# Second stages issued two slots later, and six more tiles by seven products, in a spectral-mixing and squared-ReLU kernel

## The chip, the cores and the metric

One Trainium2 chip; the kernel runs on one of its cores. The metric is the device time of one execution in microseconds (us), the median of several. Names of engines in the profile: PE is TensorE's matmul and PEld its weight load, DVE is VectorE, ACT is ScalarE, POOL is GpSimd, SP is the engine whose queue issues most transfers.

## The reference

```python
batch, seq, dim = (8, 3008, 256); d_ff = 2048
X = np.fft.rfft(x, axis=1);  Xr, Xi = X.real, X.imag
Yr = Xr @ w_r - Xi @ w_i + b_r
Yi = Xr @ w_i + Xi @ w_r + b_i
Yr = sign(Yr) * maximum(abs(Yr) - 0.01, 0);  Yi likewise
y = np.fft.irfft(Yr + 1j * Yi, n=3008, axis=1)
h = y.reshape(24064, 256) @ moe_w_in          # 256 -> 2048
r = maximum(h, 0)
out = (moe_s * (r * r) + moe_b) @ moe_w_out   # 2048 -> 256
```

## The kernel before

The first half (the transform along the sequence, the mixing, the shrinking and the transform back) is done by matmuls with constant tables, batch by batch, in units: s1 (first transform step, exits `u`), s23 (second step, mixing, shrink, first step back, exits `xf`, `ring`, `v`) and s4 (last step, exits `yt`). Between the steps data goes through HBM: `ud`, `us`, `vd`, `vs`, and the `ring` is filled by small transfers. The exits from PSUM are copies (L187 on ScalarE, L189 on VectorE).

The second half works on 48 tiles of up to 512 rows of `y` (`_tile_order`): six "wide" ones for each of batches 0 and 1, then five "main" ones per later batch, with "tail" tiles of a pair of batches between them. `mark[b] // MC` is the number of batch b's first tile, called m below: 12, 17, 23, 29, 35 and 41 for batches 2 to 7.

A tile has 16 slots (`MC`), one for each 128 of the 2048 columns. `first_mm` issues in each slot the two matmuls of `y @ w_in`, 512 columns each, into a bank of `psh`. After every second slot ScalarE takes two banks by ReLU into `rt` (L871), and `rt * rt` goes as fp16 into `gt`, on VectorE (L884) or ScalarE (L881). A planner decides which: `act_first` (L180) compares the work that it has booked on both, and it places most exit copies in the same way. `gt` has four buffers, two to a tile: `q=0` holds the squares of slots 0 to 7, `q=1` those of slots 8 to 15.

The second stage of a tile, `r * r @ w_out`, is issued beside the first stage of the next tile, slot by slot. There are two forms:

- `second_mms`: four row blocks of 128 by 16 steps, 64 matmuls of 256 columns, four to a slot; one exit for two blocks (L945).
- `seven_mms`: the rows of the tile, the columns of `w_out` and the 2048 are each halved, and the 2 x 2 block product is made from seven block products in place of eight (order index 0 to 6), 112 matmuls of 128 columns, seven to a slot. The tables `T_s` hold sums of the blocks of `w_out`. The sums of blocks of `gt` are made for each half q by `s_op`, in place: n=1 adds a21 and a22 into `s1`, n=3 puts a11 - a21 over a21, n=2 takes `s1` from a11, n=4 adds a11 to a12 with an accumulating DMA from POOL's queue (L973). The first three are on VectorE (L980). Product 3 reads `s1`, 4 the new a11, 5 the new a21, 6 the new a12. The products share PSUM banks in pairs; a tile uses four banks one after the other, and `psa` has two (in the last batch `psa` and `psf` in turn). `leave(group)` empties them on VectorE (L1012, and L1030 for one sum): group 0 after products 0 and 1, group 1 after 2, group 2 after 3 and 4, group 3 after 5 and 6. Each is one to three additions scaled by `s_bc`.

`seven(ti)` says which tiles take the second form: 17 of the 48, the two ahead of each m, three of batch 0 and 1, and the last batch's but for the tiles that are too narrow or last.

The final loop is the order of issue: in each slot the units that `plan` holds for it (s1, s23, s4 units and loads), then `first_mm`, then the second-stage matmuls of the tile before. A scheduler then moves instructions by a few places on each engine. Every engine works through its own list in order. POOL's list holds the loads of `x`, the accumulating DMAs and a copy of tails (L805).

Of the kernel before, what the change touches and what calls it, by code (L numbers as in the profile page):

```python
# [11 lines left out]
ALU = mybir.AluOpType  # L12
# [84 lines left out]
def kernel(  # L97
# [14 lines left out]
    B, S, D = x.shape  # L112
# [4 lines left out]
    MC = DFF // P  # L117
# [54 lines left out]
    def matmul(out, lhs, rhs, **how):  # L172
        if pe["on"]:
            pe["now"] += 0.0025 + int(np.prod(rhs.shape[1:])) / 2400.0
        return nc.tensor.matmul(out, lhs, rhs, **how)  # L175
# [35 lines left out]
    def sum_bank(ti):  # L211
        return any_bank() if ti >= mark[B - 1] // MC else other_bank()
# [602 lines left out]
    def sub_size(tl):  # L815
        return 4 * tl[3] if tl[0] == "wide" else P
# [105 lines left out]
    def second_mms(ti):  # L922

        tl = tiles[ti]
        size = sub_size(tl)
        nsub = -(-tl[3] * (16 if tl[0] == "wide" else 1) // size)
        hold = {}

        def mm(sub, mc):

            alone = ti == len(tiles) - 1 and sub >= 2
            h = 0 if alone else sub % 2
            if h == 0 and mc == 0:
                hold["ps"] = sum_bank(ti).rearrange("p (h e) -> p h e", h=2)
            ps = hold["ps"]
            matmul(
                ps[0:size, h, :],
                lhs_of(ti, mc, sub),
                w_out_t[:, mc, :],
                start=(mc == 0), stop=(mc == MC - 1),  # L940
            )
            if mc == MC - 1 and (alone or h == 1 or sub == nsub - 1):
                k = h + 1
                ost = opool.tile([P, 2, D], F32, name="ost", tag="ost")
                nc.vector.scalar_tensor_tensor(  # L945
                    out=ost[0:size, 0:k], in0=ps[0:size, 0:k], scalar=s_bc[0:size],
                    in1=bias_bc[0:size].unsqueeze(1).to_broadcast([size, k, D]), op0=ALU.mult, op1=ALU.add,
                )
# [12 lines left out]
    def part(ti, q, i, k):  # L961
        size = 2 * sub_size(tiles[ti])
        return gts[(ti, q)][:, i, k, :, 0:size]

    def s_op(ti, n, q):

        size = 2 * sub_size(tiles[ti])
        if n == 1:
            sums[(ti, q)] = spool.tile([P, 4, 2 * P], F16, name="s1", tag="s1")
        s1 = sums[(ti, q)][:, :, 0:size]  # L970
        a11, a12, a21, a22 = (part(ti, q, i, k) for i in range(2) for k in range(2))
        if n == 4:
            nc.gpsimd.dma_start(out=a12, in_=a11, accum_op=ALU.add)  # L973
            return
        out, a, b, op = {
            1: (s1, a21, a22, ALU.add),
            3: (a21, a11, a21, ALU.subtract),
            2: (a11, a11, s1, ALU.subtract),
        }[n]
        nc.vector.tensor_tensor(out=out, in0=a, in1=b, op=op)  # L980
        work("dve", 0.07 + size / 480.0)

    def seven_mms(ti):

        tl = tiles[ti]
        size = sub_size(tl)
        hold = {}
        left = [(0, 0), (0, 1), (1, 1), None, (0, 0), (1, 0), (0, 1)]
        firsts = (0, 2, 3, 5)
        T = T_s[0]  # L990
        right = [w_block(0, 0), w_block(1, 0), T[:, 3], T[:, 0], T[:, 1], T[:, 2], w_block(1, 1)]

        def mm(n, j, c):

            if n in firsts and j == 0 and c == 0:
                hold["ps"] = sum_bank(ti).rearrange("p (n j e) -> p n j e", n=2, j=2)
            if j == 0 and c == 0:
                hold[n] = hold["ps"][0:size, 0 if n in firsts else 1]
            q, g = divmod(c, 4)
            at = slice(j * size, (j + 1) * size)  # L1000
            if left[n] is None:
                lhs = sums[(ti, q)][:, g, at]
            else:
                lhs = gts[(ti, q)][:, left[n][0], left[n][1], g, at]
            matmul(
                hold[n][:, j], lhs, right[n][:, c],
                start=(n in firsts and j == 0 and c == 0), stop=(c == MC // 2 - 1),
                skip_group_check=True,
            )

        def add(out, of, other):
            nc.vector.scalar_tensor_tensor(  # L1012
                out=out, in0=of, scalar=s_bc[0:size], in1=other, op0=ALU.mult, op1=ALU.add
            )
            work("dve", 0.4)

        def wide(t):
            return t[0:size, 0:P].unsqueeze(1).to_broadcast([size, 2, P])

        def leave(group):  # L1020
            if group == 0:
                hold["z"] = zpool.tile([P, 2, 2, P], F32, name="zz", tag="zz")
            if group in (0, 3):
                hold["o", group] = opool.tile([P, 2, D], F32, name="ost", tag="ost")
            z = hold["z"][0:size]
            top = hold["o", 0][0:size]
            if group == 0:
                add(z[:, 0], hold[0], wide(bias_bc))
                add(top[:, :, 0:P], hold[1], z[:, 0])
                nc.vector.tensor_tensor(out=z[:, 1], in0=z[:, 0], in1=wide(b_21), op=ALU.add)  # L1030
                work("dve", 0.34)
            elif group == 1:
                add(z[:, 0], hold[2], z[:, 0])
            elif group == 2:
                add(z[:, 1], hold[3], z[:, 1])
                two = hold[4].rearrange("p j e -> p (j e)").unsqueeze(1).to_broadcast([size, 2, D])
                zs = z.rearrange("p h j e -> p h (j e)")
                add(zs, two, zs)
# [12 lines left out]
        order = [  # L1051
            (n, j, c) for h in range(2) for n in range(early) for j in range(2)
            for c in range(4 * h, 4 * h + 4)
        ]
        order += [(n, j, c) for n in range(early, 6) for j in range(2) for c in range(C)]
        order += [(6, j, c) for h in range(2) for j in range(2) for c in range(4 * h, 4 * h + 4)]
        slots = [[] for _ in range(MC)]
        for at, what in enumerate(order):
            slots[at // 7].append(lambda w=what: mm(*w))
        for at, n, q in ((2, 2, 0), (2, 1, 1), (2, 4, 0), (3, 3, 1), (4, 2, 1), (5, 4, 1)):  # L1060
            at += alone and at > 3
            slots[at].append(lambda n=n, q=q: s_op(ti, n, q))
        for at, group in ((4 + alone, 0), (6, 1), (11, 2), (15, 3)):
            slots[at].append(lambda group=group: leave(group))
        return slots

    def seven(ti):
        if ti >= len(tiles) - 2 or not halves(ti):
            return False
        firsts = [mark[b] // MC for b in range(2, B)]  # L1070
        return (
            ti >= firsts[-1] or 4 <= ti < 7 or any(m - 2 <= ti < m for m in firsts)
        )

    plan = {}
# [18 lines left out]
    mark = {}  # L1094
# [13 lines left out]
    for b in range(2, B):  # L1108
        s0, s1, s2 = mark[b - 2], mark[b - 1], mark[b]
        p = s1 - s0  # L1110
        units, take_rows = s1_units(b)
# [4 lines left out]
        units, take_half = s23_units(b)  # L1116
# [7 lines left out]
                )  # L1124

    ti_n = len(tiles)
    for ti in range(ti_n + 1):
        nxt = [[]] * MC
        if ti:
            nxt = seven_mms(ti - 1) if seven(ti - 1) else second_mms(ti - 1)  # L1130
        for mc in range(MC):
            if ti < ti_n:
                for u in plan.pop(ti * MC + mc, []):
                    u()
                first_mm(ti, mc)
                if mc in (10, 11) and seven(ti):
                    s_op(ti, 1 if mc == 10 else 3, 0)
            for u in nxt[mc]:
                u()
    assert not plan  # L1140


# [28 lines left out]
```

## Time and profile before

| what | value |
|---|---|
| median of 3 runs (lowest to highest) | 838.71 us (838.18 to 838.87) |
| the profiled execution | 838.19 us |
| its span, first to last instruction | 836.4 us |
| granted TensorE clock | 1.000 |
| chain that ended last: PE, DVE, ACT, DMA | 81%, 8%, 5%, 3% |
| `rt` by ReLU on ScalarE (L871) | 384 of 1009 ns |
| squares on VectorE (L884), on ScalarE (L881) | 254 of 1204 ns, 130 of 1037 ns |
| sums of `gt` on VectorE (L980) | 102 |
| accumulating DMAs (L973) | 34 |

The table's durations are means of one instruction. Instructions of one engine overlap in part, so that a group's busy time is less than its count by its mean. A matmul's record lasts longer than its turn: what it costs is the distance to the next one's start. In a line of the waits the three numbers are us in total, times, and the longest; in a line of the timeline, start, length, engine, line, operation, what it writes and reads, and how many follow each other; idle time before it and what ended it stand in brackets.

### The profile page before, as it was taken

How to read it: one execution, taken by the hardware profiler on the slowest of the kernel's cores; microseconds unless marked ns; L12 is line 12 of the kernel's file. 1: busy time of each engine (PE TensorE's matmuls, PEld its weight loads, DVE VectorE, ACT ScalarE, POOL GpSimd, SP SyncE). 2: the span in 40 equal slices, each digit the busy share in tenths (PEclk: the TensorE clock that was granted, in tenths of full speed). 3: DMA queues.
4: the chain of work that ended last, by engine and by line, in shares of the span. 5: the costliest groups of instructions: out<-in, count | busy, mean ns of one | idle time of the engine just before them, and what ended most of it. 6: DMA issues, size and time to landing. Idle time of an engine off the chain costs nothing.

```text
span 836.4 us, 19090 instructions
## 1 busy us (share of the span) xinstructions
PE 824.2 (99%) x7470; PEld 598.7 (72%) x7470; DVE 698.8 (84%) x1061; ACT 712.2 (85%) x953; POOL 79.8 (10%) x106
## 2 busy tenths in 40 slices
PE   8999999999999999999999999999999999999997
PEld 7857767777677767777677776777767777767765
DVE  5988989978898888877888788787889878889885
ACT  5998988998899989988899888988879888788882
POOL 4550001100011001100010000100001000001000
PEclk9999999999999999999999999999999999999999
DMA  8954578345873378534772258713565133513321
GB/s 201 183 150 103 120 181 213 64 96 132 199 185 65 98 181 198 126 88 116 192 190 65 81 131 206 180 47 97 127 177 138 48 97 90 140 45 76 72 66 61
DMA packets 115516, 105.04 MB, mean 126 GB/s; under 512 B 12646, under 2 KB 100714, under 8 KB 114082
## 3 DMA queue, kind: packets, MB, share of 16 engines
q1 hardware_dynamic: 102498, 80.55, 34.0%
q0 software_dynamic: 12928, 23.27, 17.6%
q8 instruction: 58, 0.95, 0.5%
q14 instruction: 32, 0.26, 0.1%
HBM read 53.52 MB, written 46.66 MB: 120 GB/s over the span
## 4 chain that ended last, share of the span: by engine, by line
PE 81%; DVE 8%; ACT 5%; DMA 3%; issue 2%; POOL 0%; SPq 0%; DVEq 0%; ACTq 0%; POOLq 0%
PE psh L175 33%; PE psa L175 30%; PE psf L175 17%; ACT rt L871 2%; DVE gt L884 2%; DVE gt L980 1%; DMA ring<-ring 1%; DMA x<-in_x_dram 1%; PE psm L175 1%; ACT gt L881 1%; DVE s L980 1%; DVE ost L1012 1%; ACT u L187 1%; DMA vd<-v 0%; DVE zz L1012 0%
## 5 line engine op out<-in xcount | busy, mean ns | idle before, releaser
L871 ACT ACTIVATE rt<-psh 128x1024 f32<-128x1024 f32 (+2 forms) x384 | 387.0, 1009 | 67.4 <-PE psh L175 65.2
L175 PEld LDWEIGHTS <-gt 128*128 128x128 f16 (+1 forms) x3568 | 303.7, 101 | 171.1 <-DVE gt L884 0.5
L175 PE MATMUL psh<-yt,w_in 128*128 128x512 f16 (+1 forms) x1344 | 396.5, 378 | 0.1
L884 DVE TENSOR_TENSOR gt<-rt 128x1024 f16<-128x1024 f32 (+2 forms) x254 | 304.9, 1204 | 88.6 <-ACT rt L871 86.8
L175 PE MATMUL psa<-w_out_t,gt 128*128 128x256 f16 (+3 forms) x2512 | 333.1, 258 | 0.0
L175 PEld LDWEIGHTS <-w_in 128*128 128x128 f16 x1536 | 137.3, 98 | 25.9 <-issue 3.2
L881 ACT ACTIVATE gt<-rt 128x1024 f16<-128x1024 f32 (+2 forms) x130 | 134.8, 1037 | 3.2
L187 ACT CAST u<-psf 96x512 f16<-96x512 f32 x96 | 55.7, 581 | 9.3 <-PE psf L175 8.6
L175 PE MATMUL psa<-T_s,gt 128*128 128x128 f16 (+1 forms) x752 | 63.5, 219 | 0.0
L699 DVE TENSOR_TENSOR ring<-psf,s 128x512 f16<-128x512 f32 x84 | 57.6, 685 | 4.2 <-PE psf L175 3.1
L187 ACT CAST v<-psf 128x512 f16<-128x512 f32 x82 | 47.5, 582 | 14.2 <-PE psf L175 13.3
L973 POOL DMA_DIRECT2D gt<-gt x34 | 31.1, 916 | 262.3 <-PE psh L175 86.3
L234 POOL DMA_DIRECT2D x<-in_x_dram x36 | 19.3, 540 | 386.3 <-PE psf L175 337.7
L175 PEld LDWEIGHTS <-xf 128*128 128x128 f16 x504 | 47.4, 98 | 7.2 <-DVE xf L672 1.7
L175 PE MATMUL psh<-tail,w_in 128*128 128x512 f16 (+1 forms) x192 | 52.1, 352 | 0.0
L175 PE MATMUL psf<-W_g,xf 128*128 128x256 f16 x336 | 50.4, 272 | 0.0
L945 DVE SCALAR_TENSOR_TENSOR ost<-psa,s_bc,bias_bc 128x512 f32<-128x512 f32 (+2 forms) x59 | 43.0, 730 | 4.5 <-PE psa L175 2.3
L187 ACT CAST yt<-psf 128x470 f16<-128x470 f32 (+2 forms) x84 | 43.2, 534 | 3.4 <-PE psf L175 2.2
L187 ACT CAST xf<-psf 128x512 f16<-128x512 f32 x67 | 39.1, 584 | 4.3 <-PE psf L175 4.1
L175 PE MATMUL psf<-x,A_t 94*96 94x512 f16 x102 | 38.9, 382 | 1.7 <-ACT yt L187 0.3
L175 PE MATMUL psf<-C_t,vs 96*128 96x94 f16 (+1 forms) x484 | 37.9, 205 | 0.0
L1012 DVE SCALAR_TENSOR_TENSOR ost<-psa,s_bc,zz 128x256 f32<-128x256 f32 (+1 forms) x64 | 28.8, 479 | 5.4 <-PE psa L175 3.6
(118 smaller groups left out, 758.2 us busy)
## 6 DMA issues: line engine op xcount, KB each, us to landing
out_dram<-ost SPq DMA_DIRECT2D x152, 128.0 KB
ud<-u SPq DMA_DIRECT2D x56, 192.0 KB
us<-ud SPq DMA_DIRECT2D x28, 384.0 KB
vd<-v SPq DMA_DIRECT2D x42, 256.0 KB
vs<-vd SPq DMA_DIRECT2D x14, 768.0 KB
x<-in_x_dram POOLq DMA_DIRECT2D x28, 376.0 KB, 6.5
ring<-ring SPq DMA_DIRECT2D x280, 32.0 KB
gt<-gt POOLq DMA_DIRECT2D x30, 256.0 KB, 4.6
```

The source lines that it names most:

```text
L175: return nc.tensor.matmul(out, lhs, rhs, **how)
L187: return None, nc.scalar.copy(out=dst, in_=src)
L234: nc.gpsimd.dma_start(out=t[0:N1, i * w : (i + 1) * w], in_=xv[:, c * XCH * D + i * w : c * XCH * D + (i + 1) * w],)
L699: nc.vector.tensor_tensor(out=ring[0][:, i % 4], in0=ps, in1=hold[i // 2][:, i % 2].unsqueeze(1).to_broadcast([P, 2, D]), op=ALU.add,)
L871: nc.scalar.activation(out=rt[:, :, 0:w], in_=ps[:, :, 0:w], func=AF.Relu)
L881: nc.scalar.activation(out=gt, in_=rr, func=AF.Square)
L884: last_square[0] = nc.vector.tensor_tensor(out=gt, in0=rr, in1=rr, op=ALU.mult)
L945: nc.vector.scalar_tensor_tensor(out=ost[0:size, 0:k], in0=ps[0:size, 0:k], scalar=s_bc[0:size], in1=bias_bc[0:size].unsqueeze(1).to_broad ...
L973: nc.gpsimd.dma_start(out=a12, in_=a11, accum_op=ALU.add)
L980: nc.vector.tensor_tensor(out=out, in0=a, in1=b, op=op)
L1012: nc.vector.scalar_tensor_tensor(out=out, in0=of, scalar=s_bc[0:size], in1=other, op0=ALU.mult, op1=ALU.add)
```

## The change

```diff
+    def third_last(ti):
+        return any(ti == mark[b] // MC - 3 for b in range(2, B))
+
     def s_op(ti, n, q):
...
-        if n == 4:
+        if n == 4 and not (q == 1 and third_last(ti)):
             nc.gpsimd.dma_start(out=a12, in_=a11, accum_op=ALU.add)
             return
         out, a, b, op = {
             1: (s1, a21, a22, ALU.add),
             3: (a21, a11, a21, ALU.subtract),
             2: (a11, a11, s1, ALU.subtract),
+            4: (a12, a12, a11, ALU.add),
         }[n]
...
-        for at, n, q in ((2, 2, 0), (2, 1, 1), (2, 4, 0), (3, 3, 1), (4, 2, 1), (5, 4, 1)):
+        for at, n, q in ((1, 1, 1), (2, 3, 1), (2, 2, 0), (2, 4, 0), (4, 2, 1), (5, 4, 1)):
             at += alone and at > 3
+            if third_last(ti) and at > 3:
+                at = 6 if n == 2 else 10
             slots[at].append(lambda n=n, q=q: s_op(ti, n, q))
...
-            ti >= firsts[-1] or 4 <= ti < 7 or any(m - 2 <= ti < m for m in firsts)
+            ti >= firsts[-1] or 4 <= ti < 7 or any(m - 3 <= ti < m for m in firsts)
...
-    for ti in range(ti_n + 1):
-        nxt = [[]] * MC
-        if ti:
-            nxt = seven_mms(ti - 1) if seven(ti - 1) else second_mms(ti - 1)
-        for mc in range(MC):
-            if ti < ti_n:
-                for u in plan.pop(ti * MC + mc, []):
-                    u()
-                first_mm(ti, mc)
-                if mc in (10, 11) and seven(ti):
-                    s_op(ti, 1 if mc == 10 else 3, 0)
-            for u in nxt[mc]:
-                u()
+    LAG = 2
+    behind = {}
+    for at in range((ti_n + 1) * MC + LAG):
+        ti, mc = divmod(at, MC)
+        if ti < ti_n:
+            for u in plan.pop(at, []):
+                u()
+            first_mm(ti, mc)
+        if 0 < ti <= ti_n and mc == 0:
+            mms = seven_mms(ti - 1) if seven(ti - 1) else second_mms(ti - 1)
+            for k, units in enumerate(mms):
+                behind[at + LAG + k] = units
+        for u in behind.pop(at, []):
+            u()
+        if ti < ti_n and mc in (12, 13) and seven(ti):
+            s_op(ti, 1 if mc == 12 else 3, 0)
```

A second stage begins two slots after the next tile's first stage, in place of together with it, and runs two slots into the tile after that. The sums of `gt` that are made beside it come in another order: n=1 and n=3 of q=1 first, in slots 1 and 2 of the stage. The first two sums of q=0 come after slots 12 and 13 of the tile's own first stage. Six more tiles, numbers 9, 14, 20, 26, 32 and 38 (the third before each m), take the seven products, 23 in all. In these six, n=4 of q=1 is an addition on VectorE and not a DMA, issued in slot 10 of the second stage, and n=2 of q=1 is issued in slot 6.

More of the change, by code (lines that the diff above doesn't have):

```diff
@@ L1126 @@
     ti_n = len(tiles)
-    for ti in range(ti_n + 1):
-        nxt = [[]] * MC
-        if ti:
-            nxt = seven_mms(ti - 1) if seven(ti - 1) else second_mms(ti - 1)
-        for mc in range(MC):
-            if ti < ti_n:
-                for u in plan.pop(ti * MC + mc, []):
-                    u()
-                first_mm(ti, mc)
-                if mc in (10, 11) and seven(ti):
-                    s_op(ti, 1 if mc == 10 else 3, 0)
-            for u in nxt[mc]:
-                u()
+    LAG = 2
[4 more added lines that the diff above has]
+            for u in plan.pop(at, []):
+                u()
+            first_mm(ti, mc)
[7 more added lines that the diff above has]
+            s_op(ti, 1 if mc == 12 else 3, 0)
+    assert not behind
     assert not plan
```

## The prediction

> **What bounds the kernel now.** I read the page's totals first, then TensorE's own timeline, then one batch tile by tile, then the waits and the two queues that the change adds to.
>
> ```profile
> PE 824.2 (99%) x7470; PEld 598.7 (72%) x7470; DVE 698.8 (84%) x1061; ACT 712.2 (85%) x953; POOL 79.8 (10%) x106
> ```
>
> TensorE is never long without work, but a busy share says nothing of its rate, because matmuls overlap. The rate is in the distance from one start to the next. TensorE beside a tile with seven products (first four lines) and beside a plain one (last two):
>
> ```profile
> 420.89 0.60 PE L175 MATMUL psa<-w_out_t,gt 128*128 128x256 f16 x4
> 421.33 0.59 PE L175 MATMUL psh<-tail,w_in 128*128 128x512 f16 x2
> 421.76 0.55 PE L175 MATMUL psa<-w_out_t,gt 128*128 128x128 f16 x7
> 422.15 0.37 PE L175 MATMUL psf<-C_t,vs 96*128 96x94 f16 x5
> ...
> 406.33 0.60 PE L175 MATMUL psa<-w_out_t,gt 128*128 128x256 f16 x4
> 406.76 0.38 PE L175 MATMUL psf<-ring,T_t 128*128 128x256 f16 x2
> ```
>
> Four matmuls of 256 columns take 0.44 us (421.33 less 420.89) or 0.43 (406.76 less 406.33), so 0.109 each; seven of 128 take 0.39 (422.15 less 421.76), so 0.056 each; two of 512 take 0.43. All follow each other without a gap, so a saved column is a saved time wherever nothing else is late. Whether the others keep up is read from one batch, cut at the first first-stage matmul of tiles 21, 22 and 23 (tile 23 opens batch 4). Columns: stretch, length, then busy time of PE, PEld, DVE, ACT, POOL, clock, DMA share, GB/s:
>
> ```profile
> 405.89:421.33 15.44, 15.44 (x107) 10.33 (x106) 12.47 (x13) 11.81 (x17) 0.93 (x2) 1.00 0.84 211
> 421.33:437.40 16.07, 16.04 (x210) 12.04 (x208) 14.41 (x22) 15.31 (x22) 1.88 (x3) 1.00 0.82 201
> 437.40:454.11 16.71, 16.64 (x187) 12.38 (x185) 15.38 (x30) 16.04 (x20) 2.63 (x3) 1.00 0.29 65
> ```
>
> The first stretch is the slack one: VectorE and ScalarE together work 24.3 us of 30.9. The second and third, where the seven products of tiles 21 and 22 run, are at 92% and 94%. The new seven-product tile (20) has its second stage in the slack stretch. Where today's seven-product tiles lose time, from the waits:
>
> ```profile
> PE psa L175 <- DVE ost L1012: 1.4, 4, 0.6
> ...
> PEld L175 <- DVE ost L1012: 2.0, 6, 0.5
> ```
>
> Ten waits, 3.4 us in the whole run, end when VectorE has taken the first pair of products out of its PSUM bank (group 0). One of them, timed:
>
> ```profile
> 426.84 0.68 DVE L980 TENSOR_TENSOR gt<-gt,s 128x1024 f16<-128x1024 f16 x1
> 427.44 0.48 DVE L1012 SCALAR_TENSOR_TENSOR zz<-psa,s_bc,bias_bc 128x256 f32<-128x256 f32 x1
> ...
> 428.48 0.10 PEld L175 LDWEIGHTS <-s 128*128 128x128 f16 x1 [0.20 <-DVE ost L1012]
> ```
>
> The sum at 426.84 (n=2 of the second half) stands ahead of group 0 on VectorE, and the third bank of the tile needs one of the two `psa` banks back.
>
> **The change, part by part.**
>
> *Six more tiles by seven products.* Each replaces 64 matmuls of 256 columns by 112 of 128 (the build has 288 = 6 x 48 more). From those starts: 64 x 0.109 = 6.99 us becomes 112 x 0.056 = 6.25, so 0.74 to 0.75 a tile, **-4.5 us** for six. The clock is granted in full (1.00 in every stretch), so nothing scales that.
>
> [...]
>
> *What they ask of VectorE.* Per tile six sums and, for the second half's n=4, a seventh; groups 0 to 3 in place of two L945 exits. The rows of a sum and of an exit:
>
> ```profile
> L980 DVE TENSOR_TENSOR gt<-gt,s x34: 648/683/693, 131.4 to 803.5; 128x1024 f16<-128x1024 f16 x30, 128x960 f16<-128x960 f16 x4
> ...
> L1012 DVE SCALAR_TENSOR_TENSOR ost<-psa,s_bc,zz x64: 472/478/488, 135.4 to 813.3; 128x256 f32<-128x256 f32 x56, 120x256 f32<-120x256 f32 x8
> ```
>
> A sum lasts 0.685 but the next starts 0.60 later (426.84 to 427.44), so 7 x 0.60 = 4.2 us. The exits: seven at 0.478, one double at 0.75, the plain sum of group 0 (L1030) at its median of 0.415 = 4.5, less 2 x 0.746 of L945 = +3.0. So 7.2 us more per tile, 43 in all, on an engine with 836.4 - 698.8 = 138 us idle; the planner answers in the build by giving ScalarE 12 more squares of 1.04 us and moving copies both ways. In the slack stretch land 3.0 of exits and, by the build's order, five of the seven sums (3.0): 24.3 + 6.0 = 30.3 us for two engines in 2 x (15.44 - 0.75) = 29.4. That is full and 0.9 over; with the stretch after it (29.7 of 32.1) and the next (31.4 of 33.4) the three come to 91.4 of 94.9. The cover for this work is thus used up, not exceeded on average. Price: the stretches at 92% and 94% lose 0.03 and 0.07 us of PE today, the 0.9 us over shared by two engines is 0.45 late. Ends: 0, and 6 x 1.1 = 6.6 (the whole 0.9 and a wait of 0.2 like the one shown). I take 0.3 a tile, nearer to the neighbours that run as full: **+1.8**.
>
> *Second stage two slots later, sums in another order.* q=1's first sum now precedes n=3 and n=2 of both halves, n=2 and n=1 no longer meet in one slot, and everything that reads `gt` has two slots (some 2 us) more after the squares. Group 0 stays two slots ahead of the bank's next use, but the four sums before it are spread over four slots instead of three; for the six new tiles n=2 of q=1 goes behind group 0. So the ten waits shrink. Ends: -3.4 (all gone) and +2 (VectorE comes fuller into them, 6 x 0.3). I take a third, **-1.0**. At the start the two slots without second stage leave 8 matmuls of 0.109 fewer where ScalarE is the bound (9.19 busy of the first tile's 9.20): at most +0.9, and at the end the wait of 0.2 before the last tile's exits can go: ends -0.2 and +0.9, taken **+0.3**.
>
> *Six more accumulating DMAs of 256 KB on POOL's queue* (q=0's n=4).
>
> ```profile
> 409.62 0.52 POOL L234 DMA_DIRECT2D x<-in_x_dram  x1 [10.98 <-PE psf L175]
> 420.92 0.52 POOL L234 DMA_DIRECT2D x<-in_x_dram  x1 [10.79 <-PE psf L175]
> ...
> 411.63 0.79 SPq L755 DMA_DIRECT2D vs<-vd  x2
> ```
>
> In the build the new one stands between these two x loads. It waits for its sum on VectorE (about 411 here) with only the x load of 420.92 behind it, which waits for TensorE until then anyway. It lands in 3.2 to 7.8 us (4.7 median over 34) and is read 11 slots later. But it shares the DMA engines (share 0.84) with `vs`, issued at 411.63 and read by the first C_t matmul at 422.15; 256 KB at that stretch's 211 GB/s are 1.2 us. Ends: 0, and 6 x 1.2 = 7.2 if no slack is there; today only 0.2 us of waits end with `vs`, so I take **+0.5**.
>
> Sum: -4.5 + 1.8 - 1.0 + 0.3 + 0.5 = -2.9 us. The profiled run took 838.19 (span 836.4 and 1.8 around it), so 835.3; the median of the runs lies 0.5 higher, and I say **835.5**.
>
> **Rivals.** *The whole gain arrives*: VectorE's two slots of slack absorb the new work, and most of the waits for banks go: -4.5 - 2.5 = 831.3. For it: tiles at 92 and 94% lose almost nothing. Against: three such in a row have not been seen. *Nothing to measure*: the pile-up in tiles m-2 to m costs 0.7 a tile instead of 0.3 and the DMAs 1 us: 838. *Slower*: VectorE and ScalarE enter tile m-1 already late; the s4 exits, one a slot on two `psf` banks, then stand behind sums, and TensorE, in order, waits for each bank. A fifth of the 43 us showing on TensorE is 8.6: 838.2 - 5.5 + 0.3 + 0.5 + 8.6 = 842. It decides once the pile-up costs 6.4 us in place of 1.8, 1.1 a new tile (-4.5 - 1.0 + 0.3 + 0.5 + 6.4 = +1.7). Against: the demand of 91.4 in 94.9. *Weight loads set the pace*, each 0.098 us and not hidden: 112 x 0.098 = 11.0 for 7.0, 862; seven pairs in 0.39 us all but exclude it. [...]
>
> **How the numbers follow.** Forecast (833 to 837) 0.50, whole gain 0.20, nothing to measure 0.17, slower 0.12, weight loads 0.01. What this measurement tells from no change is 0.2%, 1.7 us. Faster 0.50 + 0.20 = 0.70, same 0.17, slower 0.13. The range goes from 831.5 (which leaves out half of the whole gain, 0.08 or so) to 840.0 (which leaves out most of the slower ones, 0.10); the forecast alone has 833 to 837.
>
> **What would show it.** Right: seven starts in 0.39 us in six more tiles; the stretch that was 405.89:421.33 is 14.7 to 15.1 us long with VectorE and ScalarE above 95%; fewer than 3.4 us of waits on group 0; L945 12 fewer. Wrong: that stretch is not shorter, or the two after it grow by more than 0.5 each, with PE waiting for `psf` exits (L187, L189); or PEld waits for `vs` by more than 1 us; or the first tile's ScalarE holds TensorE for more than 0.9.

## The result, and the profile after

The changed kernel takes **862.9 us** (median of four runs, 862.04 to 864.09) where the kernel before takes 838.44 beside it (837.61 to 838.87): ratio **1.029, interval 1.028 to 1.031**. It is 24.5 us slower; the prediction said 835.5 and faster. The profiled execution took 862.04, span 860.3. Of all executions of this document one lies apart: one of five of e18, the one that was profiled, took 1731.33 us where the other four took 859.35 to 863.40, so that e18's time below is the median of the other four and its waits are not known.

The page's totals of the changed kernel:

```profile
PE 826.3 (96%) x7758; PEld 599.4 (70%) x7758; DVE 724.2 (84%) x1133; ACT 725.0 (84%) x965; POOL 86.2 (10%) x112
```

TensorE, 99% busy before, is 96% busy of a longer span: it now stands still. Of the 23.9 us between the two profiled executions 2.5 lie ahead of the first tile (which begins at 48.20 in place of 45.74), in code that the change does not edit. The batch shown before, in the changed kernel, cut at the first first-stage matmul of tiles 20, 21, 22, 23 and 24 (same columns as before):

```profile
401.62:420.35 18.73, 17.78 (x127) 12.19 (x124) 16.51 (x28) 16.30 (x22) 0.54 (x1) 1.00 0.58 151
420.35:435.44 15.09, 14.97 (x149) 10.18 (x148) 13.83 (x20) 13.00 (x16) 1.79 (x3) 1.00 0.71 157
435.44:452.84 17.40, 16.22 (x211) 12.04 (x209) 14.68 (x23) 15.70 (x25) 2.47 (x4) 1.00 0.78 183
452.84:470.22 17.38, 16.82 (x187) 12.27 (x185) 15.34 (x27) 16.30 (x21) 2.11 (x3) 1.00 0.51 129
```

The second line answers to 405.89:421.33 and is 0.35 us shorter, as predicted. The third and fourth are 1.33 and 0.67 longer, and the first, which no step of the prediction touched, is 1.11 longer (17.62 before). What TensorE waits for now, matmuls first and then their weight loads (one stall can stand in both, so the two are not added):

```profile
PE psf L175 <- DMA vs<-vd: 6.0, 3, 3.9
PE psa L175 <- DMA gt<-gt: 5.8, 6, 2.0
PE psf L175 <- DVE v L189: 5.1, 5, 1.2
PE psa L175 <- DVE ost L1016: 4.0, 11, 0.8
...
PEld L175 <- DVE ost L1016: 10.0, 16, 1.3
PEld L175 <- DMA gt<-gt: 7.0, 7, 2.2
PEld L175 <- DMA vs<-vd: 6.6, 3, 4.1
```

Before, only the group 0 waits (1.4 and 2.0 us, now L1016) were more than 0.3 us among these four. Three kinds are new, or all but new: for `vs`, for the accumulating DMAs, and for VectorE's exit of `v`. How two of them hang together, in the timeline around the first stretch's end (VectorE, TensorE, then SP's and POOL's queues):

```profile
418.26 1.23 DVE L884 TENSOR_TENSOR gt<-rt 128x1024 f16<-128x1024 f32 x1
419.40 0.68 DVE L189 CAST v<-psf 128x512 f16<-128x512 f32 x1
420.13 0.38 PE L175 MATMUL psf<-x,A_t 94*96 94x512 f16 x1 [0.95 <-DVE v L189]
...
423.28 1.27 SPq L899 DMA_DIRECT2D out_dram<-ost  x2
424.02 0.52 POOL L234 DMA_DIRECT2D x<-in_x_dram  x1 [12.04 <-PE psf L175]
424.66 0.41 SPq L744 DMA_DIRECT2D vd<-v  x1
...
431.74 0.79 SPq L755 DMA_DIRECT2D vs<-vd  x2
```

The exit of `v` stands on VectorE behind a square, and behind the copies of the `ring` and the new sums before it; TensorE waits 0.95 for the bank. In the kernel before, ScalarE makes all but 2 of the 84 exits of `v`; now VectorE makes 7. Later the last write of `vd` leaves behind two output stores and 0.64 after an `x` load, and `vs`, which reads it back, can be issued only 7.08 us after it. Before, the write (409.20) went 0.42 ahead of the `x` load (409.62) and `vs` (411.63) followed it by 2.43.

### The profile page after: what moved, and what is told of

Its sections match the earlier page's. It is cut to its first block, busy times and chain, and to the rows that moved or that the text cites. A ratio compares the mean times of both kernels' runs of the same rounds, so it can differ in the third digit from the quotient of the medians.

```text
span 860.3 us, 19791 instructions
## 1 busy us (share of the span) xinstructions
PE 826.3 (96%) x7758; PEld 599.4 (70%) x7758; DVE 724.2 (84%) x1133; ACT 725.0 (84%) x965; POOL 86.2 (10%) x112
## 4 chain that ended last, share of the span: by engine, by line
PE 63%; DVE 15%; DMA 13%; ACT 4%; issue 3%; SPq 1%; POOL 1%; DVEq 0%; POOLq 0%; ACTq 0%
PE psh L175 25%; PE psa L175 22%; PE psf L175 15%; DMA gt<-gt 5%; DVE gt L884 4%; DMA vd<-v 3%; DMA vs<-vd 3%; ACT rt L871 2%; DVE ring L699 1%; DVE gt L984 1%; DVE ring L727 1%; PE psm L175 1%; DVE ost L1016 1%; DMA x<-in_x_dram 1%; DVE ost L945 1%
## 5 line engine op out<-in xcount | busy, mean ns | idle before, releaser
L884 DVE TENSOR_TENSOR gt<-rt 128x1024 f16<-128x1024 f32 (+2 forms) x242 | 290.6, 1206 | 61.3 <-ACT rt L871 60.1
L175 PE MATMUL psa<-w_out_t,gt 128*128 128x256 f16 (+3 forms) x2416 | 300.6, 251 | 5.8 <-DMA gt<-gt 5.8
L881 ACT ACTIVATE gt<-rt 128x1024 f16<-128x1024 f32 (+2 forms) x142 | 147.5, 1039 | 3.5
L175 PE MATMUL psa<-T_s,gt 128*128 128x128 f16 (+1 forms) x1040 | 87.4, 219 | 0.0
L976 POOL DMA_DIRECT2D gt<-gt x40 | 36.6, 967 | 309.2 <-DVE gt L984 140.6
L187 ACT CAST v<-psf 128x512 f16<-128x512 f32 x77 | 44.7, 582 | 16.8 <-PE psf L175 16.7
L187 ACT CAST u<-psf 96x512 f16<-96x512 f32 x89 | 51.5, 581 | 6.4 <-PE psf L175 5.0
L1016 DVE SCALAR_TENSOR_TENSOR ost<-psa,s_bc,zz 128x256 f32<-128x256 f32 (+1 forms) x88 | 40.3, 478 | 14.9 <-PE psa L175 14.7
L187 ACT CAST xf<-psf 128x512 f16<-128x512 f32 x75 | 43.6, 585 | 4.5 <-PE psf L175 4.3
L175 PEld LDWEIGHTS <-s 128*128 128x128 f16 (+1 forms) x368 | 26.0, 101 | 21.1 <-DVE ost L1016 10.0
```

What stands on the lines that cost most here:

```text
L187: return None, nc.scalar.copy(out=dst, in_=src)
L881: nc.scalar.activation(out=gt, in_=rr, func=AF.Square)
L884: last_square[0] = nc.vector.tensor_tensor(out=gt, in0=rr, in1=rr, op=ALU.mult)
L1016: nc.vector.scalar_tensor_tensor(out=out, in0=of, scalar=s_bc[0:size], in1=other, op0=ALU.mult, op1=ALU.add)
```

## The experiments

| label | what it is | us | against before, interval |
|---|---|---|---|
| e1_lag | two slots alone | 844.89 | 1.008, 1.006 to 1.010 |
| e2_order | new order of sums alone | 840.66 | 1.002, 1.001 to 1.004 |
| e3_tiles | six tiles alone | 846.40 | 1.009, 1.007 to 1.011 |
| e4_lag_order | two slots, new order | 848.42 | 1.012, 1.008 to 1.016 |
| e10_lag_tiles | two slots, six tiles | 862.04 | 1.029, 1.027 to 1.030 |
| e5_lag_gate | e1, `x` loads held back | 849.07 | 1.013, 1.011 to 1.014 |
| e13_lag_choices | e1, planner's old choices | 843.76 | 1.006, 1.004 to 1.009 |
| e17_lag_stores | e1, stores held back | 843.37 | 1.005, 1.003 to 1.006 |
| e6_tiles_dma | e3, all n=4 by DMA | 866.52 | 1.034, 1.032 to 1.035 |
| e7_tiles_g0 | e6, sums behind group 0 | 907.46 | 1.082, 1.080 to 1.084 |
| e12_tiles_pin | e3, two sums pinned | 847.21 | 1.010, 1.009 to 1.012 |
| e14_tiles_choices | e3, old choices | 859.39 | 1.023, 1.020 to 1.026 |
| e16_pin_choices | e12, old choices | 860.26 | 1.026, 1.023 to 1.030 |
| e8_after_gate | changed, `x` loads held back | 861.15 | 1.028, 1.025 to 1.030 |
| e9_choices | changed, old choices | 849.47 | 1.013, 1.012 to 1.015 |
| e11_no_dma | changed, all n=4 on VectorE | 854.09 | 1.019, 1.018 to 1.020 |
| e15_lag_tiles_choices | e10, old choices | 852.51 | 1.016, 1.013 to 1.019 |
| e18_after_stores | changed, stores held back | 861.75 | 1.027, 1.025 to 1.029 |

The kernel before took 838.1 to 838.95 beside them. Differences below are against its time in the same set. Where a tile's stretch is named, it goes from the first matmul of the tile's first stage to that of the next tile's, as in the lines above, in the profiled execution; a tile's second stage lies in the stretch of the tile after it.

### The parts by themselves

**e1, the two slots.** The second stage is issued two slots later, the first two sums of q=0 with it; tiles and order as before.

```diff
-                if mc in (10, 11) and seven(ti):
-                    s_op(ti, 1 if mc == 10 else 3, 0)
...
+    LAG = 2
...
+                behind[at + LAG + k] = units
...
+        if ti < ti_n and mc in (12, 13) and seven(ti):
+            s_op(ti, 1 if mc == 12 else 3, 0)
```

> The kernel before with its second stages two slots later (and the first two sums of q=0 after slots 12 and 13), the sums beside the second stage in the old order, 17 tiles by seven products. Theory A (the six new tiles fill VectorE and the DMA engines at the moment when vd and vs go through HBM, and that is the loss): within 2 us of the 838.4 before, no wait of TensorE for vs over 0.5 us. Theory B (the two slots and the new order put the accumulating DMAs too late and bunch VectorE's work, in old tiles as well): at least 6 us slower, with waits of PE for the DMA gt in tiles that were there before.

It costs 6.6 us, all by itself. That is Theory B's time but not its cause: only one stall of TensorE, of 0.5 us, ends with an accumulating DMA. What neither theory named is the wait for `vs`. Here it is, with the timeline at the place shown above:

```profile
PE psf L175 <- DMA vs<-vd: 5.1, 4, 1.5
```

```profile
412.08 0.59 ACT L187 CAST v<-psf 128x512 f16<-128x512 f32 x1
412.33 1.27 SPq L899 DMA_DIRECT2D out_dram<-ost  x2
413.12 0.52 POOL L234 DMA_DIRECT2D x<-in_x_dram  x1 [10.98 <-PE psf L175]
413.70 0.42 SPq L744 DMA_DIRECT2D vd<-v  x1
...
420.84 0.79 SPq L755 DMA_DIRECT2D vs<-vd  x2
```

The same in the kernel before:

```profile
406.90 1.27 SPq L899 DMA_DIRECT2D out_dram<-ost  x2
...
408.58 0.59 ACT L187 CAST v<-psf 128x512 f16<-128x512 f32 x1
409.20 0.38 SPq L744 DMA_DIRECT2D vd<-v  x1
```

SP's list has the same order in both. Before, the stores are out (408.17) before the last `v` is (409.17), and the write leaves at once. Two slots later the stores start when `v` is nearly out (412.67), their issue takes until 413.60, and the write leaves 1.03 us late, behind an `x` load now. `vs` then follows in 7.14 us instead of 2.43, and TensorE arrives at C_t first. (Once, in batch 3, the kernel before has the same delay without harm: the load goes 1.87 ahead, `vs` follows by 7.03, and no matmul waits for it.) The group 0 waits, which the two slots were to shrink, are 1.2 us for the matmuls and 3.2 for the weight loads, where they were 1.4 and 2.0.

**e2, the order of the sums.**

```diff
-for at, n, q in ((2, 2, 0), (2, 1, 1), (2, 4, 0), (3, 3, 1), (4, 2, 1), (5, 4, 1)):
+for at, n, q in ((1, 1, 1), (2, 3, 1), (2, 2, 0), (2, 4, 0), (4, 2, 1), (5, 4, 1)):
```

> The kernel before with only the new order of the sums (n=1 and n=3 of q=1 first, one slot earlier), nothing later, 17 tiles by seven products. Theory A: within 2 us of before. Theory B in its form 'the order alone does it': the accumulating DMA of q=0 is issued some 1.2 us later (two sums of 0.6 ahead of its own), 3 us or more slower, waits for the DMA gt; in its form 'the two slots do it': within 2 us.

It is 2.4 us slower, between its two theories: the order alone brings nothing. Its group 0 waits are 1.8 and 2.4 us.

**e3, the six tiles**, in the old order and without the two slots.

```diff
-        if n == 4:
+        if n == 4 and not (q == 1 and third_last(ti)):
...
-            ti >= firsts[-1] or 4 <= ti < 7 or any(m - 2 <= ti < m for m in firsts)
+            ti >= firsts[-1] or 4 <= ti < 7 or any(m - 3 <= ti < m for m in firsts)
```

> The kernel before with only the six new tiles by seven products (n=4 of their second half on VectorE, n=2 and n=4 of it in the later slots), second stages not moved, old order. Theory A: 15 us or more slower than before, with waits of PE for vs and for v exits as in the changed kernel (5 to 7 us for vs). Theory B: TensorE's 4.5 us come through at least in part, 834 to 839 us, and no wait for vs over 1 us.

It costs 8.1 us, which neither theory expected, and no matmul waits for `vs`. The waits for group 0 are 9.1 and 8.0 us (1.4 and 2.0 before). The profiled execution took 851.12, more than the median; of what it takes more than that of the kernel before, 5.7 us lie ahead of the first tile and in tile 3's stretch, where no new tile is near.

```profile
PE psa L175 <- DVE ost L1016: 9.1, 13, 1.0
...
PEld L175 <- DVE ost L1016: 8.0, 10, 1.2
```

One of them, in a new tile (tile 20, in tile 21's stretch; it is 1.03 or 1.04 in four of the six):

```profile
419.93 0.48 DVE L1016 SCALAR_TENSOR_TENSOR zz<-psa,s_bc,bias_bc 128x256 f32<-128x256 f32 x1
420.32 0.68 DVE L984 TENSOR_TENSOR gt<-gt 128x1024 f16<-128x1024 f16 x1
420.92 0.48 DVE L1016 SCALAR_TENSOR_TENSOR ost<-psa,s_bc,zz 128x256 f32<-128x256 f32 x1
...
421.46 0.23 PE L175 MATMUL psa<-T_s,s 128*128 128x128 f16 x1 [1.03 <-DVE ost L1016]
```

The sum that the change gives to VectorE (420.32, n=4 of the second half) stands between the two additions that free the bank. The source issues it in slot 10, and the n=2 before it (419.32) in slot 6, both behind group 0, which it issues in slot 4; the scheduler has put them ahead, and does so in the changed kernel too (n=2 at 427.26, the two additions at 427.86 and 428.86, n=4 at 428.26). So this stretch, to be 0.7 shorter by the saving, is 0.47 longer than before (15.91 in place of 15.44).

**e4 and e10, two parts at a time**: the changed kernel without its six tiles, and without its order of sums. The first two lines below are e4 against the changed kernel, the other two e10.

```diff
-            ti >= firsts[-1] or 4 <= ti < 7 or any(m - 3 <= ti < m for m in firsts)
+            ti >= firsts[-1] or 4 <= ti < 7 or any(m - 2 <= ti < m for m in firsts)
...
-        for at, n, q in ((1, 1, 1), (2, 3, 1), (2, 2, 0), (2, 4, 0), (4, 2, 1), (5, 4, 1)):
+        for at, n, q in ((2, 2, 0), (2, 1, 1), (2, 4, 0), (3, 3, 1), (4, 2, 1), (5, 4, 1)):
```

> The changed kernel without its six new tiles: second stages two slots later and the new order, 17 tiles by seven products. Theory A: 838 to 842 us (the changed kernel's tiles 4 to 8, which have no new tile near them, lose 2.7 us more than before). Theory B: 850 us or more.

> The changed kernel with the old order of the sums (n=2 of q=0 first): the two slots and the six tiles together. If the parts add (6.6 us for the two slots, 8.1 for the tiles): 852 to 854 us. Theory G (the new order makes n=2 of q=0, and so its DMA, late, and both DMAs of a tile run at once): waits for the DMA gt under 2 us in all, against 12.8 in the changed kernel (PE and PEld together), 850 to 856. Rival (two slots and tiles already collide without the order): 860 us or more.

Two slots and order: +10.1, close to 6.6 + 2.4 = 9.0, and between its two theories. Two slots and tiles, as the rival of e10 has it: **+23.6, where 6.6 and 8.1 make 14.7**. These two make nearly the whole loss of 24.5, and they do not add up. In e10:

```profile
PE psf L175 <- DMA vs<-vd: 8.9, 3, 3.9
PE psa L175 <- DMA gt<-gt: 4.8, 5, 2.5
PE psf L175 <- DVE v L189: 4.1, 5, 1.0
```

### What the two slots lose

**e5.** The `x` loads wait for a copy of the last `yt` of the batch, and so come later than `vd`.

```diff
-emit_load_x(b + 1, chunks=range(c, c + 1))
+emit_load_x(b + 1, None if c else yts[b - 1][0:1, DC - 1, N2 - 1, N1 - 1 : N1], range(c, c + 1))
```

> The kernel of e1_lag (second stages two slots later, nothing else), and the x loads of the batch after next held back: the first of them waits, through a one-element copy on POOL, for the last yt exit of the batch before, so that no x load stands beside the last vd write. In e1_lag an x load was issued 0.6 us ahead of that write in batches 2, 4 and 5, and vs could be issued only 7.1 to 7.9 us after it; where the load came 0.4 us after it (before) or not at all, 2.4 to 3.8. Theory C (the two slots push the last vd write behind two stores in SP's queue, there it loses the race against the x load, and TensorE waits for vs): vs follows the write by under 4 us, waits for vs under 0.5 us in all, 838 to 841 us. Rival (the one us behind the stores is the loss, the load is not): vs waits of 3 us or more stay, 843 us or more.

The waits for `vs` are gone (`vs` follows the write by 3.05 to 4.1 us in every batch), as Theory C has it, and yet the kernel is 4.2 us slower than e1 and 8 above Theory C's range. The longest stall, 3.67 us until 167.55, ends with an accumulating DMA that was issued at 152.44, just behind three `x` loads (149.14 to 151.92), and landed at 167.51. The waits, and then the landing times of L976:

```profile
PE psa L175 <- DMA gt<-gt: 4.3, 3, 3.7
```

```profile
DMA to landing us min/median/max: 3.3/6.1/15.1
```

**e13.** The planner decides 822 times between ScalarE and VectorE. Booked two slots later, its sums change 136 of the decisions (7 in e2, 58 in e3, 169 in e10, 176 in the changed kernel). Here they are as in the kernel before.

```diff
-return max(load["act"], ready) + ta <= max(load["dve"], ready) + td + lean[0]
+return next(choice) == "1"
```

> The two slots alone (844.9, +6.6), with the 822 choices between ScalarE and VectorE that the planner makes in the kernel before; left to itself the planner makes 136 of them otherwise once the sums are booked two slots later. Theory C (the two slots cost through the planner): 838 to 840.5, VectorE's late v exits go, and the vs waits fall to 2 us or less. Theory S (they cost through the order of stores, v writes and x loads in the DMA queues, which the choices do not touch): 843 to 845.5, vs waits 4 us or more.

843.76, with 4.0 us of waits for `vs`: what Theory S expects. The planner is not what the two slots lose: 5.7 of the 6.6 us remain.

**e17.** The stores are issued three slots later, and behind the last `v` write issued.

```diff
+held.setdefault(slot[0] + 3, []).append(lambda: store_behind(tl, sub, src))
...
+with tc.issue_after(vd_last["w"].ins):
+    store_now(tl, sub, src)
```

> The two slots alone (844.9), with the output stores held back three slots and behind the last v write that was issued, so that in most batches both v writes leave SP's queue before the pair of stores. Theory S (the stores hold the last v write back by about 1 us, past the x load that was issued behind it before): the last vd write leaves within 0.2 us of its v exit, ahead of the x load again; vs follows it by 2.4 to 3.5 us; the vs waits fall from 5.1 us to under 1.5; 838.5 to 840.5. Rival (the loss lies in how long the x load and the writes share the engines, whatever their order): vs still 5 us or more behind vd, 843 to 846.

Its timeline at the same place (two writes are one line; the second leaves at about 413.6, when `v` is out):

```profile
410.01 3.96 SPq L746 DMA_DIRECT2D vd<-v  x2
...
412.98 0.59 ACT L189 CAST v<-psf 128x512 f16<-128x512 f32 x1
...
414.01 0.51 POOL L236 DMA_DIRECT2D x<-in_x_dram  x1 [10.98 <-PE psf L175]
414.06 0.62 SPq L916 DMA_DIRECT2D out_dram<-ost  x1
...
415.99 1.30 SPq L757 DMA_DIRECT2D vs<-vd  x2
```

Only the issue of the stores was edited, and the write is ahead of the `x` load again, `vs` follows it by 2.4 us here (2.35 to 2.42 in five of the seven batches), and no wait for `vs` is left among TensorE's. So the stores in SP's queue are shown to be what made `vs` late. The four stretches in which e1 waits for it (tiles 11, 16, 22 and 28) are together 5.05 us longer than before in e1, and 0.6 shorter than before in e17. The time, though, is 843.4, above the 838.5 to 840.5 expected, so that 2.2 of the 6.6 us come back. Of the rest, 2.6 us now go to the accumulating DMAs, 2.0 of them in one stall in tile 6's stretch; and what e1 loses apart from `vs` stays, 0.5 us in each of three tiles that open a batch (17.23 in place of 16.71, for one), where group 0 and the exits of `xf` are late, and 0.8 and 0.6 in the stretches of tiles 45 and 47.

### What the tiles lose

**e6 and e7.** e6 (first two lines): the new tiles' second n=4 goes by DMA too, so that VectorE has six sums. e7 (the rest): beside that, three sums go behind group 0.

```diff
-        return any(ti == mark[b] // MC - 3 for b in range(2, B))
+        return False
...
-        for at, n, q in ((2, 2, 0), (2, 1, 1), (2, 4, 0), (3, 3, 1), (4, 2, 1), (5, 4, 1)):
+        for at, n, q in ((2, 1, 1), (5, 2, 0), (5, 4, 0), (6, 3, 1), (7, 2, 1), (8, 4, 1)):
...
+            with tc.issue_after(hold["g0"].ins):
+                s_op(ti, n, q)
```

> The kernel of e3_tiles (six more tiles, nothing later), with every n=4 as an accumulating DMA: no fourth sum on VectorE and the slots of the other tiles for n=2 and n=4. In e3_tiles the build puts that VectorE sum between the two additions of group 0. Theory D (that sum delays group 0): the waits for group 0 in the new tiles go from 1.2 us to about 0.6, 841.5 to 844.5 us. Rival (the VectorE sum spares the DMA engines more than it costs): waits for vs or for the DMA gt of 1.5 us or more, 846 us or more.

> The kernel of e6_tiles_dma, with n=2 of both halves and n=3 of q=1 tied on VectorE behind the second addition of group 0, in all seven-product tiles (only n=1 of q=1 stays ahead). Theory E (group 0 is late because four sums stand ahead of it, and this eats the gain of the tiles): TensorE's waits for group 0 fall from 17 us in e3_tiles to under 5, 833 to 838 us. Rival (VectorE is full in these tiles whatever stands first): the waits move to the sums, to the DMA gt or to the psf exits, 841 us or more.

In e6 and then in e7, the wait that grew:

```profile
PE psa L175 <- DMA gt<-gt: 19.3, 5, 5.0
```

```profile
PE psa L175 <- DMA gt<-gt: 44.0, 21, 7.8
...
PE psa L175 <- DVE ost L1016: 1.2, 5, 0.3
```

e7 shows the exchange: group 0 waits fall to 1.2 us for the matmuls and 3.8 for the weight loads, about what Theory E has, but the time is 69 us above its range; a sum that lets group 0 pass starts its DMA later than TensorE needs it. Of e6's two expectations the rival holds. The half of n=4 on VectorE, with its later slots, is worth 20 us to these tiles: without it the stretches of tiles 10, 21, 27, 33 and 39 are 3.1 to 6.2 us longer than before, with it (e3) 0.47 or 0.48.

**e12, e14 and e16.** e12: n=2 of the second half goes behind group 0 in all tiles, and the new tiles' n=4 behind group 1. e14 and e16: e3 and e12 with the old choices (edit as in e13).

```diff
+            key = {(2, 1): "g0", (4, 1): "g1"}.get((n, q))
...
+            with tc.issue_after(hold[key].ins):
+                s_op(ti, n, q)
```

> The kernel of e3_tiles (six more tiles, nothing later, old order), with n=2 of q=1 tied on VectorE behind group 0's second addition in all seven-product tiles and the VectorE n=4 of the new tiles tied behind group 1. n=2 of q=0, and so the early DMA, stays where it was. Theory E in this smaller form (two sums ahead of group 0 cost the new tiles 1.2 us each, and nothing else is wrong with them): waits for group 0 under 6 us against 17.1, 836 to 841 us. Rival (VectorE and ScalarE are simply full): the waits move to other exits or to the second DMA, 844 us or more.

> The six tiles alone (846.4, +8.1), with the choices of the kernel before; left to itself the planner makes 58 of them otherwise. Theory G (what the tiles lose, they lose behind group 0 on VectorE): 845 to 848, and the waits for group 0 stay at 8 us or more. Theory C (the changed choices are half of it): 840 to 843, and the waits for group 0 fall below 5 us.

> The six tiles alone with the sums pinned behind groups 0 and 1 (847.2), with the choices of the kernel before. Left to itself the planner makes 81 otherwise. Theory C: the waits for the accumulating DMAs (5.4 us), which took the place of the group 0 waits, go too, and the time is 838 to 842, the first with six tiles that comes near the kernel before. Theory D (the new tiles' second DMA is late in itself): 845 to 848 with those waits at 4 us or more.

e12 takes most of the group 0 waits away and gains nothing in all; waits for the accumulating DMAs take their place, as its rival has it:

```profile
PE psa L175 <- DMA gt<-gt: 5.4, 5, 1.3
PE psa L175 <- DVE ost L1016: 2.3, 5, 0.6
```

But tile 21's stretch, first in e3 and then in e12, shows what the total hides (columns as before):

```profile
413.68:429.59 15.91, 14.88 (x155) 10.26 (x154) 14.30 (x21) 14.18 (x19) 1.82 (x3) 1.00 0.87 194
410.38:425.17 14.79, 14.79 (x154) 10.25 (x153) 14.36 (x21) 13.99 (x19) 1.81 (x3) 1.00 0.85 196
```

With the two sums behind groups 0 and 1 TensorE does not stand still in it, and the saving is there: it is 0.65 shorter than before, and the stretches of tiles 10, 27 and 33 are 0.73 shorter (tile 39's is as before). VectorE and ScalarE do as many instructions in both, 21 and 19. So in these stretches it is the place of the sums that takes the saving away. What e12 loses lies elsewhere: 4.85 us in the stretches of tiles 5, 42, 43, 44 and 46, where no new tile is and where its edit moves n=2 of the old ones too, and 3.0 in tile 11's, where 1.3 us each are waited for `vs` and for an accumulating DMA. A run that pins the sums in the six new tiles alone was not made.

e14 and e16 come out 13 us worse than with the planner's own choices, outside all their expectations. In e14 the matmuls' group 0 waits stay (9.2 us; the weight loads' fall from 8.0 to 2.6) and 3.8 us for the DMAs are added.

So the changed choices are not what the tiles lose; without the two slots they are what the planner saves. The waits shown do not account for the full 13 us.

### What the changed kernel loses

**e8, e11 and e18.** e8: the gate of e5. e11: every n=4 on VectorE behind group 1, no accumulating DMA at all (its edit is shown). e18: the stores as in e17.

```diff
-        if n == 4 and not (q == 1 and third_last(ti)):
-            nc.gpsimd.dma_start(out=a12, in_=a11, accum_op=ALU.add)
-            return
...
-        for at, n, q in ((1, 1, 1), (2, 3, 1), (2, 2, 0), (2, 4, 0), (4, 2, 1), (5, 4, 1)):
+        for at, n, q in ((1, 1, 1), (2, 3, 1), (2, 2, 0), (10, 4, 0), (4, 2, 1), (10, 4, 1)):
```

> The changed kernel, with the x loads held back as in e5_lag_gate. Theory C: the three waits for vs (1.0, 1.4 and 4.1 us) and the half-clock stretch after the longest go, 852 to 856 us against 862.9. Rival (the accumulating DMA beside vd is enough without the load): vs still follows the last vd write by more than 5 us, 859 us or more.

> The changed kernel without any accumulating DMA: every n=4 on VectorE, behind group 1. If the DMAs' landing (3.3 to 9.8 us) is what holds TensorE for gt and helps to hold it for vs: no wait for the DMA gt, vs waits under 3 us, 850 to 856 us. Rival (the 40 additional sums of 0.6 us on a full VectorE cost what the DMAs did): 860 us or more, with more waits for group 0.

> The changed kernel (862.9) with the same hold on the stores. Theory S, if the order of the stores is what starts the vs waits there too: they fall from 6.0 to under 2 us and 855 to 859 remains. If it is the late v exits on VectorE (1.1 us in each batch) that start them, vd is not earlier and the time stays at 861 to 864.

e8 again moves the wait: none for `vs`, 8.9 us for the DMAs (5.8 before the gate), 861.15; neither of its expectations has both the wait and the time. e11 is 8.8 us faster than the changed kernel, in the range that it was given, and no wait for an accumulating DMA is left; but 4.5 us for `vs` (under 3 were expected) and 5.1 for the `v` exits are. The 8.8 us are not the price of 40 DMAs against 40 sums alone: with the sums booked on VectorE, the planner also gave ScalarE 21 more squares (163 for 142). e18 gives back little if anything: it is 22.8 us above the kernel before in its set, for 24.5, and the two intervals overlap. In the changed kernel, too, two stores hold the last `v` write back, by 1.03 to 1.06 us in four of seven batches; yet holding them back decides little here. Why is open, since the waits of e18 are not known.

**e9 and e15.** The changed kernel, and e10, with the old choices (edit as in e13).

> The changed kernel, with the planner's choices of engine for exits and squares taken over one by one from the kernel before (176 of its 822 choices were others). Theory F (the planner, misled by the shifted bookings, put v exits on VectorE behind ring copies, and four waits of TensorE of 1.1 us end on them): those four waits go, 857 to 860 us against 862.9. Rival (the choices matter little, or VectorE with more squares makes group 0 later): 862 us or more.

> Two slots and six tiles together (862.0, +23.6, where the two alone add up to 14.7), with the choices of the kernel before (169 differ otherwise). If the part that does not add up (8.9 us) is made by the planner, this lands at the sum of the two other runs of this set: within 2 us of 838.4 plus their two excesses. If it is made by the transfers (vs and the accumulating DMAs sharing the engines), it lies 5 us or more above that sum.

e9 gets back **13.4 of the 24.5 us**, more than Theory F expected and three times the 4.5 of the late exits by themselves (the stretches of tiles 9, 20, 26 and 32, 1.11 or 1.12 each). Its waits:

```profile
PE psa L188 <- DVE ost L1031: 8.0, 8, 1.3
PE psa L188 <- DMA gt<-gt: 2.4, 3, 1.1
...
PE psf L188 <- DMA vs<-vd: 1.1, 1, 1.1
```

The waits for `v` are gone, and with them most of those for `vs` and the DMAs; the matmuls' group 0 waits are larger (8.0 for 4.0), the weight loads' smaller (3.3 for 10.0). By stretches, e9 is 4.5 us shorter at the late exits, and 5.7 in that of tile 11 (16.39 for 22.10), where the changed kernel has its longest stall for `vs`; it is 4.5 longer in those of tiles 10, 21, 27 and 33, where it waits 1.26 for group 0 each time, and 2.0 shorter ahead of the first tile, which differs from run to run (45.7 to 49.7 us in the traces). e15 gets back 9.2 of e10's 23.6 us. With the choices fixed, two slots (5.7) and tiles (21.3) together cost 14.4, 12.6 less than their sum; with the planner free, 8.9 more than their sum. Neither expectation of e15 holds. So the choices decide how far the two parts differ from their sum, and in which direction; that they do not add up is true with fixed choices too. Why a given set of choices fits one arrangement and not another was not settled.

## Why the prediction was wrong

**The saving was right.** In the new tiles seven starts follow in 0.39 us (429.67 to 430.06), L945 has 12 fewer (39 of the main form for 51), and weight loads set no pace. Where nothing is late all of the saving shows: 0.73 us in three of e12's stretches, 0.74 to 0.75 forecast. In the changed kernel 0.35 of it is left, and the stretch forecast at 14.7 to 15.1 us is 15.09; but VectorE and ScalarE are 89% busy in it (26.83 of 30.18), not over 95%. Two of the prediction's signs of being wrong came: weight loads wait 6.6 us for `vs`, and the two stretches after it grew by more than 0.5 each, though not by waits for exits: TensorE's longest wait in them is for `vs` (0.86), and its waits for the exits of `v` lie ahead of them.

**The step that failed is "second stage two slots later", taken at -1.0 with ends of -3.4 and +2.** Alone it is +6.6. The step counted the sums and banks that get two slots, and not the output stores that are issued with it. They moved against the last `v` write on SP's queue, which the prediction read only for `vs`; e1's timeline and e17 show it for the waits for `vs`. Nor does its premise hold that in the new tiles n=2 of q=1 goes behind group 0: the scheduler puts it ahead. Nor did the expected gain come: the ten waits for group 0, 3.4 us, are eight of 4.4 us in e1, ten of 4.2 with the new order alone (e2), and 14.0 in the changed kernel. e17 leaves 4.4 of the 6.6 us, which the lateness of `vs` does not explain.

**The pile-up on VectorE, +1.8, was mis-sized.** By the prediction's terms the six tiles alone are -4.5 + 1.8 + 0.5 = -2.2; e3 gives +8.1. The wait shown in e3 is 1.03 us, and as long in four of the new tiles; 0.3 was taken. An average demand of 91.4 in 94.9 us said that the work fits; it did not say where it stands, and a sum between two additions is enough; e12's stretches show the saving whole, with VectorE and ScalarE as busy in them, once that sum stands elsewhere. By the same terms e3 leaves 8.1 + 4.5 - 0.5 = 12.1 us for the pile-up, 2.0 a new tile. The slower rival asked for 1.1 and had the direction, but the wrong place: in e3 TensorE waits for `psa`, not for `psf`.

**The accumulating DMAs, +0.5 with an upper end of 7.2, were mis-sized.** Without any of them, and with the planner's answer to that, e11 is 8.8 us faster than the changed kernel. The term thought of `vs` alone; as much is waited for the sums themselves (5.8 us for 6.0). The two longest of these waits, 1.4 and 2.0 us, end with DMAs that took 9.8 and 8.9 us to land:

```profile
DMA to landing us min/median/max: 3.3/5.4/9.8
```

Before, these were 3.2, 4.7 and 7.8.

**The sum itself failed.** It added terms as if each stood alone. The two main parts do not add up: 14.7 us apart, 23.6 together. And the planner, named in the prediction for 12 more squares, remade 176 of 822 choices; its `v` exits on VectorE, which no term had, make 0.95 of the 1.11 us by which the first stretch shown grew. (One slip changes nothing: 835.3 and the 0.5 by which the median lies higher are 835.8, not 835.5.)

The rivals of a whole gain and of nothing to measure fell with these steps; that of the weight loads, near in its number (862) by chance alone, fell with the starts. The start and the end (+0.3) had no run of their own, but e1's trace has them: tile 0's stretch is 9.21 us as before, tile 1's 0.60 shorter, and the last one 0.58 longer, so that nothing was lost at the start and the end did not gain. No version with one of the three parts came out faster than the kernel before.

## What to carry to other kernels

A step that is moved takes its stores along: read each queue it issues to, and see which other transfer comes to stand behind them. Read the order of instructions from the built kernel's trace, not from the source, where a scheduler stands between. When two parts of a change draw on the same slack, price them together, and by the place of single instructions, not by the average load. Where a total does not move, compare it stretch by stretch: e12's 8.8 us hide four stretches in which the saving is there. Where a planner decides from booked costs, replay its old decisions under the new order: that separates the change from what the planner made of it, but the old ones may fit worse.

## What the hardware showed

**Half the clock behind a stall.** TensorE waits 3.94 us for `vs` before 240.31 in the changed kernel. Windows behind it, and after that (columns as before, the clock third from the end):

```profile
240.60:244.10 3.50, 3.50 (x30) 2.64 (x27) 1.96 (x4) 2.07 (x3) 0.00 (x0) 0.52 1.00 236
244.20:248.00 3.80, 3.80 (x54) 2.95 (x52) 3.02 (x5) 3.45 (x6) 0.00 (x0) 1.00 0.20 70
```

For 3.5 us the granted clock is 0.52, so that the stall costs an estimated 1.7 us more than itself (3.5 x 0.48). The length of a stall does not decide alone here. In the same trace the clock is 0.50 from 15.50 to 18.70, behind a stall of 1.84 us (until 14.69), and a stall of 2.03 us, until 744.10, is followed by the full clock (1.00 from 744.15 to 747.60).

**0.6 us ahead or 0.4 behind.** Where an `x` load went 0.58 us (e1) or 0.64 us (the changed kernel) ahead of the last `vd` write, at the places shown, `vs` followed the write by 7.14 and 7.08 us; where the load went 0.42 behind it (the kernel before), by 2.43, though the two are on different queues (POOL's and SP's). With the loads held back (e5) it is 3.05 to 4.1, and with the write ahead again (e17) 2.35 to 2.42 in five of seven batches. So the read behind the write that came second started 4.7 us later (7.14 for 2.43).

**One kind of transfer, 3.2 to 15.1 us.** The accumulating DMA of 256 KB lands in 3.2 us at best in the kernel before and in 15.1 in e5, issued just behind three loads of `x`; the medians are 4.7 and 6.1.
